# Attention with a gated feed-forward block on one core: loads and emission order redone

## The chip, the cores and the metric

One core of one Trainium2 chip runs the whole program. The metric is device time in microseconds (us). Every time quoted is a median of executions in the fast state. Traces are of one execution each, and their span (first to last instruction) is some 1.8 us below the time of that execution. Engines: PE is TensorE, PEld its weight loads, DVE VectorE, ACT ScalarE, POOL GpSimd, SP SyncE.

## The reference

```python
# q, k, v: (8, 8, 576, 64); phi: (8, 8, 576, 32)   [cut to what matters]
a = softmax(phi, axis=2)                     # over the 576 tokens, for each of 32 memory slots
k_m, v_m = a^T @ k, a^T @ v                  # per head 32 x 64
attn = softmax(q @ k_m^T / 8) @ v_m
x = attn in tokens x (heads * 64)            # 4608 x 512
out = (silu(x @ w_gate) * (x @ w_val)) @ w_out   # d_ff = 1536
```

The code works on eight batches of 576 tokens. For each it computes: the key/value sums ("sums"), the scores and their exponentials, the denominators, U = v_m @ w (so that the feed-forward input is never formed), 24 "slots" of gate and value matmuls with silu and multiply, and 54 output matmuls on average. In the kernels the softmax of phi runs over the tokens, with its denominator divided out of the sums. A U round (`u_round`) makes one piece of U of 512 columns, in eight matmuls and two copies. The exp chain is what stands between the scores and the first slot of a batch: exponentials, denominators and the division. In the profile lines t_qT is the transposed q, t_h the product of silu and value, t_A the divided exponentials, p_g and p_v the banks that scores, gates and values share, p_oo that of the outputs; L12 is line 12 of that kernel's file.

## The kernel before

```python
    def load_qT(b):

        t = att.tile([128, H, 3, P], BF16, tag="qT", name="t_qT")
        nc.sync.dma_start_transpose(
            out=t.rearrange("p h j t -> p (h j) t"),
            in_=qs[b].rearrange("p h f -> p (h f)"),
        )
        for i in range(NP):
            qTs[b, i] = t[:, 2 * i:2 * i + 2].rearrange("p h j t -> p h (j t)")
    # [cut]
    def load_w(which, c):
        src = (moe_w_gate, moe_w_val)[which]
        t = wpool.tile([128, NP, CH], BF16, tag=f"W{which}{c}", name=f"W{which}{c}")
        nc.gpsimd.dma_start(
            out=t, in_=src[:, c * CH:(c + 1) * CH].rearrange("(i p) f -> p i f", p=128)
        )
        W[which, c] = t
    # [cut: load_wo, key/value sums, q_T, scores, z_norm]
    def u_round(b, which, c):
        p = [ps.tile([128, CH], FP32, tag="s", name=f"p_u{g}") for g in range(NG)]
        for i in range(NP):
            for g in range(NG):
                nc.tensor.matmul(
                    p[g][32 * i:32 * i + 32, :],
                    lhsT=kTs[b][64 * g:64 * g + 64, 2, 32 * i:32 * i + 32],
                    rhs=W[which, c][64 * g:64 * g + 64, i],
                    start=True,
                    stop=True,
                    tile_position=(64 * g, 32 * i),
                )
        for g in range(NG):
            t = upool.tile([128, CH], BF16, tag=f"U{which}{c}{g}", name="t_U")
            if g == 0:
                nc.scalar.copy(out=t, in_=p[g])
            else:
                nc.vector.tensor_copy(out=t, in_=p[g])
            Us[b, which, c, g] = t
    # [cut]
    def gv_slot(b, s):
        jf, r = s // 2, s % 2
        c, o = jf // 4, jf % 4
        if b % 2 == 0 and r == 0:
            hts[b // 2, jf] = hpool.tile([128, 2 * S], BF16, tag=f"h{jf}", name="t_h")
        p = gv_banks()
        for which in range(2):
            for g in range(NG):
                nc.tensor.matmul(
                    p[which][:, 0:HALF],
                    lhsT=Us[b, which, c, g][:, 128 * o:128 * (o + 1)],
                    rhs=atts[b, g][:, r],
                    start=(g == 0),
                    stop=(g == NG - 1),
                )
        sg = work.tile([128, HALF], BF16, tag="sg", name="t_sg")
        nc.scalar.activation(out=sg, in_=p[0][:, 0:HALF], func=AF.Silu)
        flush_mul()
        col = (b % 2) * S + r * HALF
        dst = hts[b // 2, jf][:, col:col + HALF]

        def mul():
            nc.vector.tensor_tensor(out=dst, in0=sg, in1=p[1][:, 0:HALF], op=ALU.mult)

        pend.append(mul)
    # [cut: out_units, out_list]
    def att_items(b):
        q = [(330, lambda i=i: q_T(b, i)) for i in range(NP)] if b == 0 else []
        return (
            [(1000, lambda: (kv_half(b, 0), kv_half(b, 1), kv_sums(b)))]
            + q[:2]
            + [(200, lambda: kv_T(b))]
            + q[2:]
            + ([] if b == 0 else [(0, lambda: load_qT(b))])
        )
    # [cut]
    def window(b, fill, nxt_phi):
        lead = min(4, len(fill))
        run(fill[:lead])
        fill = fill[lead:]
        exp_tables()
        for g in range(NG):
            scores(b, g)
        if nxt_phi:
            phi_exp(b + 1)
        cut = len(fill) // 3
        run(fill[:cut])
        for g in range(NG):
            z_norm(b, g)
        run(fill[cut:])
    # [cut]
    backlog = []
    hold = {1: 0, 2: 12, 3: 12, 4: 14, 5: 14, 6: 16, 7: 0}
    for b in range(1, B):
        if b > 1 and b + 1 < B:
            load_phi(b + 1, nc.gpsimd)
            load_kv(b + 1)
            load_q(b + 1)
        n = min(36, len(backlog))
        window(b, backlog[:n], b > 1 and b + 1 < B)
        backlog = backlog[n:]
        keep = hold[b]
        rest, backlog = backlog[:len(backlog) - keep], backlog[len(backlog) - keep:]
        slots = [lambda s=s: gv_slot(b, s) for s in range(2 * NJF)]
        if b == 1:
            interleave(slots[:12], [])
            flush_mul()
            exp_tables()
            phi_exp(2)
            interleave(slots[12:], att_items(2) + u_items(2))
        else:
            nxt = att_items(b + 1) + u_items(b + 1) if b + 1 < B else []
            interleave(slots, rest + nxt)
        flush_mul()
        backlog += out_list(b)
    run(backlog)
```

q enters the scores transposed. For batch 0 PE transposes it; for batches 1 to 7 a DMA transpose (`load_qT`) does, issued by SP. GpSimd issues the other loads. The emission order is the order of each engine, but GpSimd may run ahead as far as buffers and semaphores let it.

The softmax here doesn't subtract the row's maximum and nothing guards it: scores larger than these inputs give would overflow.

## Time and profile before

| | before |
|---|---|
| time, median | 311.6 us (3 runs, 310.5 to 312.6) |
| PE busy | 253.5 us, 82% of the span |
| ACT, DVE busy | 175.3 and 154.2 us |
| PE waits for a DMA transpose | 11.2 us, once |
| start of the scores of batches 1 to 7, us | 77.1, 108.6, 139.0, 170.0, 202.3, 232.8, 265.0 |

How to read it: PE does nearly the same work in any order, so time is gained where PE stands still or runs at half clock. The starts of the scores, read from the timeline, cut the run into batches; from 108.6 to 265.0 a batch takes 31.3 us. The lines themselves are in the prediction, but for one from the list of who waited for whom (us in total, times, longest): the value matmul's wait for a multiply.

```profile
PE p_v L277 <- DVE t_h L291: 10.0, 27, 0.5
```

### The profile page before, as it was taken

How to read it: one execution, taken by the hardware profiler on the slowest of the kernel's cores; microseconds unless marked ns; L12 is line 12 of the kernel's file. 1: busy time of each engine (PE TensorE's matmuls, PEld its weight loads, DVE VectorE, ACT ScalarE, POOL GpSimd, SP SyncE). 2: the span in 40 equal slices, each digit the busy share in tenths (PEclk: the TensorE clock that was granted, in tenths of full speed). 3: DMA queues.
4: the chain of work that ended last, by engine and by line, in shares of the span. 5: the costliest groups of instructions: out<-in, count | busy, mean ns of one | idle time of the engine just before them, and what ended most of it. 6: DMA issues, size and time to landing. Idle time of an engine off the chain costs nothing.

```text
span 309.9 us, 5844 instructions
## 1 busy us (share of the span) xinstructions
PE 253.5 (82%) x2272; PEld 140.3 (45%) x2272; DVE 154.2 (50%) x326; ACT 175.3 (57%) x364; POOL 31.4 (10%) x46
## 2 busy tenths in 40 slices
PE   0278889520697899889988999999889998989994
PEld 0234454200353446534653466446544664456641
DVE  0135762330354736673667265836673567356520
ACT  4155672240866695569556944696569546845500
POOL 8222201100103010101010102000000000000000
PEclk9999999855588999999999999999999999999999
DMA  8999999999606933899399646945102270121133
GB/s 156 203 206 207 227 204 241 271 146 156 107 2 130 177 89 91 103 152 180 87 143 149 133 103 110 191 104 116 31 2 68 70 112 3 34 78 29 42 96 97
DMA packets 47499, 37.53 MB, mean 121 GB/s; under 512 B 18160, under 2 KB 41968, under 8 KB 47472
## 3 DMA queue, kind: packets, MB, share of 16 engines
q0 software_dynamic: 24576, 23.01, 45.6%
q1 hardware_dynamic: 22896, 14.16, 23.1%
q8 instruction: 17, 0.28, 0.4%
q14 instruction: 10, 0.08, 0.1%
HBM read 42.47 MB, written 9.44 MB: 167 GB/s over the span
## 4 chain that ended last, share of the span: by engine, by line
PE 65%; DVE 11%; DMA 10%; ACT 10%; issue 3%; POOL 0%; SPq 0%; DVEq 0%; ACTq 0%; POOLq 0%
PE p_oo L315 29%; PE p_v L277 14%; PE p_g L277 10%; PE p_u L245 7%; DMA t_qT<-t_q 6%; DMA t_q<-in_q_dram 4%; DVE t_h L291 4%; ACT t_U L256 3%; DVE t_U L258 3%; ACT t_lz L233 1%; ACT t_E L223 1%; PE p_kv L138 1%; ACT t_lz L232 1%; DVE t_o L327 1%; PE p_g L213 1%
## 5 line engine op out<-in xcount | busy, mean ns | idle before, releaser
L315 PE MATMUL p_oo<-WO,t_h 128*128 128x512 bf16 x432 | 109.7, 379 | 0.7 <-DVE t_o L327 0.7
L285 ACT ACTIVATE t_sg<-p_g 128x288 bf16<-128x288 f32 x192 | 77.5, 412 | 56.4 <-PE p_g L277 44.4
L291 DVE TENSOR_TENSOR t_h<-t_sg,p_v 128x288 bf16<-128x288 bf16 x192 | 83.9, 450 | 37.1 <-ACT t_sg L285 30.1
L277 PEld LDWEIGHTS <-t_U 128*128 128x128 bf16 x768 | 73.5, 100 | 61.2 <-issue 29.2
L277 PE MATMUL p_v<-t_A,t_U 128*128 128x288 bf16 x384 | 81.4, 295 | 10.9 <-DVE t_h L291 10.0
L277 PE MATMUL p_g<-t_A,t_U 128*128 128x288 bf16 x384 | 82.1, 296 | 3.5 <-DVE t_A L235 2.6
L315 PEld LDWEIGHTS <-t_h 128*128 128x128 bf16 x432 | 41.3, 98 | 39.9 <-issue 2.6
L256 ACT CAST t_U<-p_u 128x512 bf16<-128x512 f32 x48 | 28.1, 586 | 28.6 <-PE p_u L245 28.6
L258 DVE CAST t_U<-p_u 128x512 bf16<-128x512 f32 x48 | 33.2, 692 | 20.1 <-PE p_u L245 20.1
L235 DVE TENSOR_TENSOR t_A<-t_E,t_lz 128x576 bf16<-128x576 bf16 x16 | 12.1, 759 | 41.9 <-ACT t_lz L233 41.9
L327 DVE COPY t_o<-p_oo 128x512 f32<-128x512 f32 x28 | 19.1, 689 | 27.0 <-PE p_oo L315 27.0
L245 PE MATMUL p_u<-W,t_kT 64*32 64x512 bf16 x384 | 24.8, 421 | 9.1 <-ACT t_U L256 7.0
L245 PEld LDWEIGHTS <-t_kT 64*32 64x32 bf16 x384 | 8.4, 90 | 23.9 <-issue 19.4
L138 PE MATMUL p_kv<-t_kv,t_ephi 96*32 96x128 bf16 x384 | 7.6, 231 | 14.1 <-DMA t_kv<-in_v_dram 12.6
L223 ACT ACTIVATE t_E<-p_g 128x288 bf16<-128x288 f32 x16 | 6.6, 414 | 20.4 <-PE p_v L213 20.3
L124 ACT ACTIVATE t_ephi<-t_phi 96x768 bf16<-96x768 f32 x16 | 12.6, 844 | 3.8 <-DMA t_phi<-in_phi_dram 3.8
L213 PE MATMUL p_g<-t_qT,t_kT 64*32 64x288 bf16 x64 | 5.5, 324 | 11.3 <-DMA t_qT<-t_q 11.2
L377 ACT ACT_TABLE_LOAD x11 | 14.1, 1283 | 0.9 <-PEq L470 0.7
L325 ACT COPY t_o<-p_oo 128x512 f32<-128x512 f32 x8 | 4.7, 587 | 17.5 <-DMA out_dram<-t_o 9.8
L138 PEld LDWEIGHTS <-t_ephi 96*32 96x32 bf16 x384 | 6.0, 102 | 16.2 <-issue 14.2
L160 DVE RECIPROCAL t_rS<-p_kv 128x2 f32<-128x2 f32 x8 | 1.4, 170 | 21.2 <-PE p_kv L152 21.2
L72 POOL DMA_DIRECT2D t_kv<-in_k_dram x8 | 6.3, 785 | 54.1 <-PE p_kv L138 49.8
(37 smaller groups left out, 116.3 us busy)
## 6 DMA issues: line engine op xcount, KB each, us to landing
t_kv<-in_k_dram POOLq DMA_DIRECT2D x8, 576.0 KB, 11.3
t_kv<-in_v_dram POOLq DMA_DIRECT2D x8, 576.0 KB, 13.4
t_q<-in_q_dram POOLq DMA_DIRECT2D x8, 576.0 KB, 11.1
out_dram<-t_o SPq DMA_DIRECT2D x24, 192.0 KB, 2.3
t_phi<-in_phi_dram POOLq DMA_DIRECT2D x7, 576.0 KB, 6.6
out_dram<-t_o SPq DMA_DIRECT2D x24, 128.0 KB, 2.4
W<-in_moe_w_gate_dram POOLq DMA_DIRECT2D x3, 512.0 KB, 17.3
W<-in_moe_w_val_dram POOLq DMA_DIRECT2D x3, 512.0 KB, 19.1
```

The source lines that it names most:

```text
L124: nc.scalar.activation(out=t[:, :, g].rearrange("p j i m -> p i j m"), in_=src[:, g], func=AF.Exp)
L138: nc.tensor.matmul(pk[32 * i:32 * i + 32, 2 * D * g:2 * D * (g + 1)], lhsT=ephis[b][:, j, g, i], rhs=kvs[b][:, :, 2 * i + g, j * D:(j + 1) ...
L235: nc.vector.tensor_tensor(out=a, in0=e, in1=lz, op=ALU.mult)
L245: nc.tensor.matmul(p[g][32 * i:32 * i + 32, :], lhsT=kTs[b][64 * g:64 * g + 64, 2, 32 * i:32 * i + 32], rhs=W[which, c][64 * g:64 * g + 64 ...
L256: nc.scalar.copy(out=t, in_=p[g])
L258: nc.vector.tensor_copy(out=t, in_=p[g])
L277: nc.tensor.matmul(p[which][:, 0:HALF], lhsT=Us[b, which, c, g][:, 128 * o:128 * (o + 1)], rhs=atts[b, g][:, r], start=(g == 0), stop=(g = ...
L285: nc.scalar.activation(out=sg, in_=p[0][:, 0:HALF], func=AF.Silu)
L291: nc.vector.tensor_tensor(out=dst, in0=sg, in1=p[1][:, 0:HALF], op=ALU.mult)
L315: nc.tensor.matmul(mine["p"], lhsT=hts[c, jf][:, 128 * u:128 * (u + 1)], rhs=WO[jf], start=(jf == 0), stop=(jf == NJF - 1),)
L327: nc.vector.tensor_copy(out=t_o, in_=mine["p"])
L377: nc.scalar.preload_act_table_set("natural_log_exp_and_others")
```

## The change

It sends the loads in another order with W in halves, transposes q of batch 1 on PE, keeps U in single buffers that are filled just in time, emits a value matmul one slot after its gate, spreads output matmuls over the slots and the exp chain, and puts dummy matmuls into the start.

```diff
-    upool = ctx.enter_context(tc.tile_pool(name="upool", bufs=2))
+    upool = ctx.enter_context(tc.tile_pool(name="upool", bufs=1))
[cut: load_kv split into load_k and load_v]
+    HC = CH // 2
+    def load_w(which, c, half):
+
         src = (moe_w_gate, moe_w_val)[which]
-        t = wpool.tile([128, NP, CH], BF16, tag=f"W{which}{c}", name=f"W{which}{c}")
+        if half == 0:
+            W[which, c] = wpool.tile(
+                [128, 2, NP, HC], BF16, tag=f"W{which}{c}", name=f"W{which}{c}"
+            )
+        f0 = c * CH + half * HC
         nc.gpsimd.dma_start(
-            out=t, in_=src[:, c * CH:(c + 1) * CH].rearrange("(i p) f -> p i f", p=128)
-        )
-        W[which, c] = t
+            out=W[which, c][:, half],
+            in_=src[:, f0:f0 + HC].rearrange("(i p) f -> p i f", p=128),
+        )
 
     WO = {}
[cut: key and value sums split in two for batches 0 and 1; z_norm split into z_inv and norm]
-    def gv_slot(b, s):
+    def gv_half(b, s, which):
[cut]
+        gate = gv_half(b, s, 0)
         sg = work.tile([128, HALF], BF16, tag="sg", name="t_sg")
-        nc.scalar.activation(out=sg, in_=p[0][:, 0:HALF], func=AF.Silu)
+        nc.scalar.activation(out=sg, in_=gate, func=AF.Silu)
         flush_mul()
         col = (b % 2) * S + r * HALF
         dst = hts[b // 2, jf][:, col:col + HALF]
 
         def mul():
-            nc.vector.tensor_tensor(out=dst, in0=sg, in1=p[1][:, 0:HALF], op=ALU.mult)
+            val = gv_half(b, s, 1)
+            nc.vector.tensor_tensor(out=dst, in0=sg, in1=val, op=ALU.mult)
 
         pend.append(mul)
[cut]
+    def spread(*streams):
+
+        keyed = []
+        for o, (items, first, last) in enumerate(streams):
+            for i, x in enumerate(items):
+                keyed.append((first + (i + 0.5) * (last - first) / len(items), o, i, x))
+        for _, _, _, x in sorted(keyed, key=lambda t: t[:3]):
+            x()
[cut]
+    def warm(n):
+
+        p = ps.tile([128, DM], FP32, tag="o", name="p_oo")
+        for _ in range(n):
+            nc.tensor.matmul(p[:, 0:128], lhsT=bones, rhs=bones, start=True, stop=True)
[cut]
     load_phi(0, nc.sync)
-    load_kv(0)
+    load_k(0)
+    load_phi(1, nc.gpsimd)
     load_q(0)
-    make_identity(nc, ident)
+    load_v(0)
     nc.vector.memset(bones, 0.0)
     nc.vector.memset(ones1, 1.0)
     for h in range(4):
         nc.vector.memset(bones[32 * h:32 * h + 32, 32 * h:32 * h + 32], 1.0)
+    make_identity(nc, ident)
     for c in range(NCH):
-        for which in range(2):
-            load_w(which, c)
+        for half in range(2):
+            for which in range(2):
+                load_w(which, c, half)
+    load_phi(2, nc.gpsimd)
+    load_k(1)
+    load_q(1)
+    load_v(1)
     for c in range(3):
         load_wo(c)
-    load_phi(1, nc.gpsimd)
-    load_kv(1)
-    load_q(1)
+
 
     exp_tables()
     phi_exp(0)
-    run(att_items(0))
-    window(0, [], False)
-    u0 = u_items(0)
[cut: batch 0]
+    run(q_items(1)[:2] + k_items(1)[2:] + q_items(1)[2:])
+    load_k(2)
+    load_v(2)
[cut]
+            uw = u_items(b, "vv")
+            exp_tables()
+            run(take(2))
+            for g in range(NG):
+                scores(b, g)
+            run(take(6) + uw[2:3] + take(4))
+            if not last:
+                phi_exp(b + 1)
+            for g in range(NG):
+                z_inv(b, g)
+            nc.scalar.preload_act_table_set("silu_and_others")
+            run(take(4) + uw[3:4] + take(4))
+            norm(b, 0)
+            norm(b, 1)
+            run(take(8))
+        rest = take(len(backlog)) if last else take(len(backlog) - 28)
+        g = gv_slots(b)
+        streams = [(g, 0, 24), (rest, 0, 24)]
         if b == 1:
-            interleave(slots[:12], [])
-            flush_mul()
-            exp_tables()
-            phi_exp(2)
-            interleave(slots[12:], att_items(2) + u_items(2))
+            streams += [(u1[2:4], 1, 6), (u1[4:], 8, 14)]
         else:
-            nxt = att_items(b + 1) + u_items(b + 1) if b + 1 < B else []
-            interleave(slots, rest + nxt)
+            streams += [(u_items(b)[4:], 1, 8)]
+        if not last:
+            kvn = kv_items(b + 1)
+            streams += [
+                (kvn, 12, 17) if b == 1 else (kvn, 9, 15),
+                ([lambda: load_qT(b + 1)], 16, 17),
+                (u_items(b + 1)[:2], 18, 24),
+            ]
+        spread(*streams)
         flush_mul()
         backlog += out_list(b)
     run(backlog)
```

## The prediction

> **What bounds the kernel now.** I read four views in this order. First the page: slices of the span and the shares of the chain.
>
> ```profile
> span 309.9 us, 5844 instructions
> PE 253.5 (82%) x2272; PEld 140.3 (45%) x2272; DVE 154.2 (50%) x326; ACT 175.3 (57%) x364; POOL 31.4 (10%) x46
> ...
> PE   0278889520697899889988999999889998989994
> ...
> PEclk9999999855588999999999999999999999999999
> DMA  8999999999606933899399646945102270121133
> ...
> PE 65%; DVE 11%; DMA 10%; ACT 10%; issue 3%; POOL 0%; SPq 0%; DVEq 0%; ACTq 0%; POOLq 0%
> ```
>
> TensorE is the bound, but not everywhere. A slice is 7.75 us: PE is almost idle in the first two and again in the ninth and tenth (62 to 77 us), and just there the granted clock is 0.5. The DMA engines are full until about 78 us. The second view, the chain of waits from 56 to 78 us, and the third, the list of who waited for whom, name the hole:
>
> ```profile
> 57.03 19.98 DMA t_qT<-t_q
> ...
> 77.05 0.39 PE p_g L213
> ```
>
> ```profile
> PE p_g L213 <- DMA t_qT<-t_q: 11.2, 1, 11.2
> ```
>
> Batch 1's transposed q is made by a DMA transpose that takes 20.0 us; the median of the seven is 10.2 and the quickest 5.0. PE waits 11.2 us for it. The fourth view is the busy time by stage, here 66-77, 77-93, then a stretch of gate/value slots and an output stretch of a later batch:
>
> ```profile
> 66.00:77.00 11.00, 0.00 (x0) 0.00 (x0) 0.61 (x1) 1.76 (x2) 0.00 (x0) 0.50 1.37 144
> 77.00:93.00 16.00, 12.25 (x76) 7.18 (x75) 6.97 (x14) 11.81 (x25) 0.78 (x1) 0.67 0.38 62
> ...
> 118.00:138.00 20.00, 17.94 (x210) 10.95 (x208) 13.51 (x31) 11.66 (x29) 1.53 (x2) 1.00 0.81 113
> 138.00:149.00 11.00, 11.00 (x79) 5.48 (x72) 5.44 (x9) 9.30 (x17) 1.55 (x2) 1.00 0.87 175
> ```
>
> The columns are duration, busy us of PE, PEld, DVE, ACT, POOL, then clock, DMA share, GB/s. In 138-149, where output matmuls stand beside the exp chain, PE never stops. In 118-138 it has holes, which the timeline places at each U round:
>
> ```profile
> 129.51 0.41 PE L277 MATMUL p_g<-t_A,t_U 128*128 128x288 bf16 x2
> 130.28 0.41 PE L277 MATMUL p_v<-t_A,t_U 128*128 128x288 bf16 x2 [0.36 <-DVE t_h L291]
> 130.62 0.41 PE L245 MATMUL p_u<-W,t_kT 64*32 64x512 bf16 x8
> ```
>
> Value matmuls wait for a bank that a multiply frees, and the multiply stands behind a 0.69 us U copy. The period of "two slots and a U" is 1.95 us (128.67 to 130.62), the PE work in it 2 x 0.49 + 0.34 = 1.32.
>
> **What the Trainium skill says.** "TensorE: Matmul & The Clock Gate", Part 1 and "HAM oscillation": an idle window of about 3.4 us puts the clock at half, and a busy window restores it. The trace agrees: 0.50 in 66-77, and pairs of slots take 0.96 us instead of 0.49 until 87. "DMA: Bandwidth & Descriptors", "Queues, rings and completion order": each of the 16 engines goes round robin between queues by packet, and work already queued on another queue is therefore shared with, not passed. The trace agrees: 5.0 us with nothing else under way, 20.0 us beside the loads of batches 2 and 3. "ScalarE: Activation LUTs", "What ACT_TABLE_LOAD costs": about 1283 ns for the load itself; the trace has 1.28 us.
>
> **Unit costs on PE**, all from the trace at full clock. Output matmul 0.216 (48 in 10.37 us, chain of waits from 45.11). A slot 0.49 (four matmuls, 0.245 per pair). U round 0.34 (128.67 to 129.01). Key/value sums 1.1 (125.13 to 126.23) and transposes 0.3. Scores and denominators 1.05 a batch (the gaps 139.08 to 139.63 and 141.90 to 142.38 between output stretches).
>
> **Part 1, the start.** Landings before, issue plus time to landing: k0 9.6, v0 12.5, q0 15.4, the six W by 30.7, WO by 38.3, q1 49.7, k2 55.3, v2 59.7, q2 66.3. Steps are 2.9 us for a k, v or q, about 2.6 for a phi, 2.55 for a W or WO; this is a stream at full rate. The change sends the same bytes in another order. I estimate: q0 15, v0 18, W halves (I take 1.28 each) 20 to 33.5, phi1 now early, phi2 36, k1 39, q1 42, v1 45, WO 47.5 to 52.5, k2 55.5, v2 58, q2 61. The dummy matmuls keep the clock up while PE waits for q0. Before, the first silu of batch 0 is at 27.2 and its slots end at 45. After, v0 (18) and the first W half (20) still stand in PE's order ahead of the denominators, so the first silu is near 25; a group of four slots with two half U's costs DVE 4 x 0.49 + 2 x 0.4 = 2.8 us, so 24 slots take about 17 and end near 42.
>
> **Part 2, batch 1.** q is transposed on PE, so the 20 us transfer is off this place. Its chain (exp table 1.28, phi exp 1.57, copies, exps 1.3, log and exp 2.7, two U rounds with 4 x 0.69 of copies on DVE) from 42 puts its first slot near 52, against 82 before: 30 us earlier. But output matmuls that filled 45 to 55 move too. Only 20 of the first 48 are put beside batch 1's slots and 28 are held. So not all of the 30 us is won.
>
> **Part 3, batch 2, where I expect the wait to come back.** Its q is still transposed by DMA. The order of SP shows it behind the stores of the first output tile, which completes at the 12th of 20 output matmuls, about slot 14: 52 + 14 x 0.85 = 64. GpSimd runs ahead with loads: at 64 to 65 the queue still has part of v3, q3, phi4, and k4, v4 as soon as batch 2's sums free their buffer: 2 + 2.9 + 2.6 + 2.9 + 2.9 = 13.3 us of loads. With 5 us for the transpose that is 18 to 20, as for the 20.0 of before. It lands near 85. The slots of batch 1 (24 x 0.49 + 20 x 0.216 + 4 x 0.34 + 1.4 + two U rounds 0.7 = 19.5, some 21 with bubbles) end near 74 and two output matmuls later PE stands in order before the scores of batch 2: about 10 us idle, and a half clock after it. Before, these scores were at 108.6, with 52 output matmuls done; now at 85 with 22 done. Net of 30 x 0.216 = 6.5 that is 17 us won, not 24.
>
> **Part 4, batches 2 to 7.** PE work from 85 on: 410 outputs x 0.216 = 88.6; 144 slots x 0.49 = 70.6; 34 U rounds x 0.34 = 11.6; sums 5 x 1.4 = 7; scores 6 x 1.05 = 6.3. Sum 184. The end (last copy and store, 305.6 to 309.9 before) is 4.3. Losses: before, 138.1 to 264.1 holds four batches of which PE's work is 4 x 16.2 + 212 x 0.216 = 111, so 3.8 a batch was lost. In the change the value is one slot behind its gate, so its multiply finds the silu done; outputs are spread over all slots, so U rounds stand beside them. I leave 0.3. In the window the ACT chain is table 1.3 + exps 1.3 + phi 1.6 + logs 2.6 + table 1.3 = 8.1, against 28 x 0.216 + 1.05 + 0.68 = 7.8 of PE work: 0.5 lost. So 0.8 x 6 = 5, and 3 for the half clock after the wait. Later DMA transposes are issued at slots 9 to 14 and have at least 9 us; I count nothing.
>
> 85 + 184 + 4.3 + 5 + 3 = 281 of span; the runs before are 1.7 above their span: 283. I add 1 for small stalls: **284 us**.
>
> **Rivals.** (a) The transpose of batch 2 is not in the way: if its loads are issued later or share better, scores come at 75 and the time is about 274. For it: uncontended it takes 5 us. Against: the DMA is full until the loads have caught up, and nothing in the change thins it. (b) The half chunks halve the bytes per run to 512; if the engines pay per run, W takes 4 to 5 us more and all behind it moves: 288 to 290. The spacing of 768 and 1024 byte runs (2.9 us for 576 KB, 2.55 for 512) is by bytes, against it. (c) Single U buffers and both copies on DVE make DVE the bound: DVE has 17 us in slots of 20, so it would cost 1 to 2 a batch: 290 to 296. (d) All steady losses vanish and the start goes as planned: 268 to 272.
>
> **Range and chances.** (a) and (d) set the low end, 271; (b) with (c) the high end, 296. For no gain, 27 us of stall would have to be new, and I see no place: faster by over 2% has 0.97.
>
> **What would show it.** Right: the granted clock full until about 45; first slot of batch 1 near 52; a PE wait of 6 to 13 us for the DMA transpose before batch 2's scores near 75 to 86, with half clock; then a period of 28 to 29 us a batch instead of 31; the value matmul's wait for the multiply gone. Wrong if that transpose lands by 75 (faster), if the W halves land later than 36, if PE waits for DVE in the slots, or if later transposes hold up scores.

## The result, and the profile after

292.75 us median (291.5 to 294.9, 4 runs) against 311.06 for the kernel before beside it: ratio 0.941 (95% interval 0.934 to 0.949). A second measurement gave 294.02 against 312.24 (three fast runs; 294.75 with a fourth that was slow), ratio 0.9415. The prediction was 284 with a range of 271 to 296.

The page of the changed kernel: span, busy shares, the 40 slices of 7.3 us, and the chain by engine.

```profile
span 293.0 us, 6428 instructions
PE 254.7 (87%) x2504; PEld 148.6 (51%) x2538; DVE 165.9 (57%) x350; ACT 168.6 (58%) x354; POOL 36.0 (12%) x52
...
PE   7587997699439998599959999799999999999993
...
PEclk9655999799959999689997999999999999999999
DMA  7999999999979179572797439970512251211233
...
PE 64%; DMA 23%; ACT 6%; DVE 3%; issue 2%; POOL 0%; ACTq 0%; POOLq 0%
```

The one deep hole of before has become several: PE falls in slices 11 and 12, in 17 and in 21, and each time the clock falls with it or just after. DMA has gone from 10% to 23% of the chain. (Slice 1 shows 7 because of the dummies.) The list of who waited for whom:

```profile
PE p_g L274 <- DMA t_qT<-t_q: 17.0, 4, 8.3
PE p_g L349 <- DVE t_A L303: 4.0, 4, 1.6
...
PE p_u L316 <- DVE t_U L333: 0.9, 2, 0.7
```

17.0 us in four waits for a transposed q: 8.3, 3.9, 3.3 and 1.6. The value matmul's wait for the multiply, 10.0 us in 27 waits before, has gone from the list. The chain of waits has the four transposes: start, length.

```profile
70.52 14.54 DMA t_qT<-t_q
...
105.01 15.44 DMA t_qT<-t_q
...
144.46 9.45 DMA t_qT<-t_q
...
173.01 13.75 DMA t_qT<-t_q
```

They are those of batches 2 to 5. What GpSimd issues at the second of them:

```profile
104.51 0.77 POOL L72 DMA_DIRECT2D t_kv<-in_k_dram  x1 [15.06 <-PE p_kv L149]
105.27 0.77 POOL L76 DMA_DIRECT2D t_kv<-in_v_dram  x1
```

The sums of batch 3 free a key/value buffer, and the two loads that waited for it start in the same microsecond as the transpose. Busy time by stage (length, then busy us of PE, PEld, DVE, ACT, POOL, clock, DMA share, GB/s): the wait of batch 2, its slots, the wait of batch 3.

```profile
77.00:85.20 8.20, 0.10 (x8) 0.11 (x16) 0.07 (x1) 0.65 (x1) 0.00 (x0) 0.79 1.13 139
94.50:116.00 21.50, 21.11 (x220) 13.51 (x222) 14.82 (x33) 12.46 (x30) 1.53 (x2) 1.00 0.69 97
116.00:120.50 4.50, 0.60 (x8) 0.11 (x5) 0.72 (x2) 1.20 (x1) 0.00 (x0) 0.88 0.83 127
```

In the slots PE is busy 21.1 of 21.5 us; before, it was 17.9 of 20 in a like stretch. The timeline of PE at a U round shows how:

```profile
98.59 0.41 PE L349 MATMUL p_v<-t_A,t_U 128*128 128x288 bf16 x2
98.84 0.38 PE L396 MATMUL p_oo<-WO,t_h 128*128 128x512 bf16 x1
...
99.15 0.41 PE L316 MATMUL p_u<-W,t_kT 64*32 64x512 bf16 x8
99.49 0.39 PE L396 MATMUL p_oo<-WO,t_h 128*128 128x512 bf16 x1
99.72 0.41 PE L349 MATMUL p_g<-t_A,t_U 128*128 128x288 bf16 x2
99.96 0.41 PE L349 MATMUL p_v<-t_A,t_U 128*128 128x288 bf16 x2
```

None has a bracket, which would give idle time before it; the prediction's like lines of the kernel before have 0.36 us of wait just before the U round.

### The profile page after: what moved, and what is told of

It is laid out like the page before. It is cut to its first block, busy times and chain, and to the rows that moved or that the text cites. A ratio compares the mean times of both kernels' runs of the same rounds, so it can differ in the third digit from the quotient of the medians.

```text
span 293.0 us, 6428 instructions
## 1 busy us (share of the span) xinstructions
PE 254.7 (87%) x2504; PEld 148.6 (51%) x2538; DVE 165.9 (57%) x350; ACT 168.6 (58%) x354; POOL 36.0 (12%) x52
## 4 chain that ended last, share of the span: by engine, by line
PE 64%; DMA 23%; ACT 6%; DVE 3%; issue 2%; POOL 0%; ACTq 0%; POOLq 0%
PE p_oo L396 25%; DMA t_qT<-t_q 18%; PE p_g L349 15%; PE p_v L349 13%; PE p_u L316 5%; DMA t_q<-in_q_dram 4%; PE p_kv L149 2%; ACT t_lz L297 2%; PE p_g L274 1%; ACT L563 1%; DVE t_U L333 1%; ACT t_lz L298 1%; DVE t_A L303 1%; PE p_q L251 1%; PE p_kv L161 1%
## 5 line engine op out<-in xcount | busy, mean ns | idle before, releaser
L396 PE MATMUL p_oo<-WO,t_h 128*128 128x512 bf16 x398 | 119.6, 393 | 2.1 <-issue 1.0
L372 DVE TENSOR_TENSOR t_h<-t_sg,p_v 128x288 bf16<-128x288 bf16 x192 | 86.6, 454 | 45.7 <-PE p_v L349 42.1
L349 PE MATMUL p_v<-t_A,t_U 128*128 128x288 bf16 x384 | 79.6, 291 | 0.1
L333 DVE CAST t_U<-p_u 128x512 bf16<-128x512 f32 (+1 forms) x70 | 42.9, 632 | 13.4 <-PE p_u L316 12.7
L331 ACT CAST t_U<-p_u 128x512 bf16<-128x512 f32 (+1 forms) x38 | 20.1, 530 | 10.9 <-PE p_u L316 10.4
L316 PE MATMUL p_u<-W,t_kT 64*32 64x512 bf16 (+1 forms) x432 | 23.2, 381 | 1.6 <-DVE t_U L333 0.9
L82 POOL DMA_DIRECT2D t_q<-in_q_dram x8 | 6.2, 773 | 60.0 <-DMA t_qT<-t_q 56.4
L297 ACT ACTIVATE t_lz<-p_g 128x288 f32<-128x288 f32 x16 | 6.4, 402 | 8.9 <-PE p_g L294 8.8
L460 PE MATMUL p_oo<-bones 128*128 128x128 bf16 x98 | 10.0, 295 | 1.5 <-DVE bones L471 1.5
L298 ACT ACTIVATE t_lz<-t_lz 128x576 f32<-128x576 f32 x16 | 10.9, 684 | 0.5
```

What stands on the lines that cost most here:

```text
L297: nc.scalar.activation(out=lz[:, r], in_=p[r][:, 0:HALF], func=AF.Ln)
L298: nc.scalar.activation(out=lz, in_=lz, func=AF.Exp, scale=-1.0)
L316: nc.tensor.matmul(p[g][32 * i:32 * i + 32, f0:f1], lhsT=kTs[b][64 * g:64 * g + 64, 2, 32 * i:32 * i + 32], rhs=w, start=True, stop=True, ...
L331: nc.scalar.copy(out=t[:, f0:f1], in_=p[g][:, f0:f1])
L333: nc.vector.tensor_copy(out=t[:, f0:f1], in_=p[g][:, f0:f1])
L349: nc.tensor.matmul(p[:, 0:HALF], lhsT=Us[b, which, c, g][:, 128 * o:128 * (o + 1)], rhs=atts[b, g][:, r], start=(g == 0), stop=(g == NG - 1),)
```

## The experiments

Twelve measurements (eleven kernels and the change once more), in three sets of four. The first two sets ran on one chip, the third on another, each with runs of the kernel before beside it (medians 311.3 to 312.2); the first two rows are from the measurement of the change. Starts of the scores (us, from the timelines), the time and the ratio to before:

| kernel | batch 1 | 2 | 3 | 4 | 5 | 6 | 7 | time | ratio (95%) |
|---|---|---|---|---|---|---|---|---|---|
| before | 77.1 | 108.6 | 139.0 | 170.0 | 202.3 | 232.8 | 265.0 | 311.06 | 1 |
| after | 46.6 | 85.1 | 120.5 | 154.0 | 186.8 | 214.3 | 244.4 | 292.75 | 0.941 (0.934-0.949) |
| qT_early | 44.9 | 84.7 | 117.2 | 144.8 | 174.9 | 202.5 | 232.6 | 282.24 | 0.902 (0.895-0.909) |
| qT_early_from_b2 | 44.4 | 83.8 | 116.3 | 143.9 | 174.0 | 201.6 | 231.7 | 280.79 | 0.898 (0.890-0.905) |
| q2_on_pe | 44.7 | 76.6 | 107.4 | 138.0 | 170.7 | 198.3 | 228.3 | 277.22 | 0.887 (0.880-0.894) |
| value_with_gate | 44.2 | 83.7 | 117.0 | 148.5 | 180.4 | 209.2 | 239.8 | 289.24 | 0.925 (0.918-0.932) |
| loads_held_back | 44.5 | 74.2 | 104.2 | 131.9 | 161.9 | 189.5 | 219.6 | 270.32 | 0.864 (0.857-0.872) |
| q2_on_pe_qT_early | 45.2 | 77.3 | 107.3 | 134.9 | 165.0 | 192.6 | 222.7 | 272.90 | 0.873 (0.866-0.879) |
| no_warm | 43.5 | 84.4 | 116.0 | 146.4 | 178.4 | 205.9 | 235.9 | 288.35 | 0.923 (0.915-0.931) |
| outputs_bunched | 43.8 | 82.7 | 114.4 | 143.0 | 173.4 | 201.9 | 232.3 | 286.00 | 0.912 (0.904-0.921) |
| after_again | 44.5 | 84.4 | 119.0 | 151.5 | 184.1 | 211.6 | 241.7 | 294.02 | 0.9415 (0.936-0.947) |
| held_back_no_warm | 45.9 | 76.2 | 106.3 | 133.9 | 164.0 | 191.6 | 221.6 | 272.55 | 0.873 (0.871-0.876) |
| held_back_value_with_gate | 45.7 | 78.8 | 109.4 | 138.2 | 168.8 | 197.7 | 228.2 | 277.73 | 0.889 (0.885-0.892) |
| before_q1_on_pe | 68.1 | 100.7 | 131.3 | 162.1 | 194.4 | 224.9 | 257.2 | 304.33 | 0.975 (0.972-0.978) |

All results were correct.

**Theory:** what keeps the change from its steady rate is that a DMA transpose shares the DMA engines with key and value loads that are in the queue, and PE stands before the scores until it lands. **Rival:** the transpose is slow of itself, or SP issues it too late.

### qT_early: the transpose at slot 0

```diff
-                ([lambda: load_qT(b + 1)], 16, 17),
+                ([lambda: load_qT(b + 1)], 0, 1),
```

> The DMA transpose of the next batch's q is emitted at slot 0 instead of slot 16.5, so it no longer starts together with the key and value loads that the key/value sums release. My theory (the transpose shares the DMA engines packet by packet with those loads, and PE stands before the scores until it lands): the waits before the scores of batches 3, 4 and 5 (8.7 us in the changed kernel) vanish, that of batch 2 shrinks from 8.3 to about 3, and the half clock after each goes too; about 275 us against 293, the ratio to before near 0.885. Rival (the transpose is slow of itself or the SP queue holds it wherever it stands): the waits stay near 17 us and the time within 2 of 293.

282.24 us, 7 above the expectation. The waits of batches 3 to 5 are gone: those transposes land 5.0 to 6.6 us after issue instead of 9.4 to 15.4. But batch 2's did not come earlier. The list of waits, and the chain:

```profile
PE p_g L274 <- DMA t_qT<-t_q: 9.6, 1, 9.6
```

```profile
61.72 22.91 DMA t_qT<-t_q
```

It is issued 8.8 us earlier than in the changed kernel and lands at 84.6 instead of 85.1. So the theory holds for batches 3 to 5, and the size for batch 2 was wrong: with loads queued ahead and behind, the place of the transpose in the order hardly counted. What stretches it is counted under loads_held_back.

### qT_early_from_b2: the same, batch 2 left alone

```diff
+                ([lambda: load_qT(b + 1)],) + ((16, 17) if b == 1 else (0, 1)),
```

> The same, but batch 2's transpose is left where it was. My theory: batch 2's wait of 8 us stays, those of batches 3 to 5 vanish (8.7 us and some 3 of half clock): about 281 us. If the wait of batch 2 is what sets all the later ones (a delay that is handed on), they stay: 290 or more.

280.79, as expected. Batch 2's wait is 9.2 us, the others are gone: a wait is not handed on, and the early issue did nothing for batch 2.

### q2_on_pe: batch 2's q on TensorE

```diff
-        pq = ps.tile([128, NG, HALF], BF16, tag="gv"[i % 2], name="p_q")
+        pq = ps.tile([128, NG, HALF], BF16, tag=("s" if b > 1 else "gv"[i % 2]), name="p_q")
...
+                (q_items(2), 18, 22) if b == 1 else ([lambda: load_qT(b + 1)], 16, 17),
```

> Batch 2's q is transposed on TensorE in the last slots of batch 1 instead of by DMA; all else as in the change. My theory: the 8.3 us wait before the scores of batch 2 is replaced by about 1 us of PE work, and its half clock goes: about 283 us, with the waits of batches 3 to 5 still there. Rival (PE would wait there for the loads anyway): q lands at about 63 us, slot 18 is at about 70, so no wait for it; if there is one, the time stays near 290.

277.22, 6 us better than expected. The scores of batch 2 start at 76.6 instead of 85.1. The expectation had left the waits of batches 3 to 5 as they were; here they are 3.8 us in two instead of 8.7 in three.

### value_with_gate and held_back_value_with_gate: one part undone

```diff
         gate = gv_half(b, s, 0)
+        val = gv_half(b, s, 1)
         sg = work.tile([128, HALF], BF16, tag="sg", name="t_sg")
...
         def mul():
-            val = gv_half(b, s, 1)
```

> Undoes one part: value matmuls are issued in the same slot as their gate, as before. By my prediction the value's wait for the multiply comes back: up to 0.6 us for each U round that stands in slots, 4 a batch, so up to 2.4 us a batch or 14 us in all; 300 to 307 us. Rival (the output matmuls spread over the slots fill that time anyway, and the DMA waits absorb what is left): within 3 us of 293.

289.24: undoing the part made the kernel faster than the change at 292.75 (and its repetition at 294.02, on another chip). The list of waits says why this says nothing on the part itself:

```profile
PE p_g L274 <- DMA t_qT<-t_q: 10.1, 3, 6.4
...
PE p_v L349 <- DVE t_h L372: 1.4, 5, 0.3
```

The waits for transposes fell from 17.0 to 10.1 us as slots and transposes met at other moments, which hides what the part is worth. So it was undone once more in loads_held_back (below), where no such wait is left:

> loads_held_back with the value matmuls back in the slot of their gate. In the undisturbed pairs of batches value_with_gate took 59.4 us against 57.7 (scores to scores), 0.85 a batch; over six batches 5 us: 275 to 276. If the part is worth nothing: 270. If my prediction's size for it was right (1.5 to 2.4 a batch): 279 to 284.

277.73, ratio 0.889 against 0.864 with the part. From the scores of batch 3 to those of batch 7 there are 118.9 us here (109.35 to 228.20), and 115.4 in loads_held_back (104.24 to 219.60): 0.9 us a batch. The slots of batch 1 add about 2.4 (52.4 to 78.0 against 50.0 to 73.2, by the first and last gate or value matmul). So the part is worth about 0.9 us a batch in the steady stage, less than the 1.5 to 2.4 of my prediction's size, and in the change as it stands none of it is visible.

### loads_held_back: one buffer for k, v and q

```diff
-        t = inp.tile([P, 2, H, J * D], BF16, tag="kv", name="t_kv")
+        t = inp.tile([P, 2, H, J * D], BF16, tag="kv", bufs=1, name="t_kv")
...
-        t = inp.tile([P, H, J * D], BF16, tag="q", name="t_q")
+        t = inp.tile([P, H, J * D], BF16, tag="q", bufs=1, name="t_q")
...
-                ([lambda: load_qT(b + 1)], 16, 17),
+                ([lambda: load_qT(b + 1)], 0, 1),
```

> Key/value and q tiles get one buffer instead of two, so batch 3's loads cannot start before batch 2's data are used up, and batch 2's transpose, emitted at slot 0, has the DMA engines nearly to itself from about 62 to 67 us. In qT_early, with two buffers, it was issued at 61.7 and landed at 84.6. My theory (it is the backlog of loads in the queue that stretches it): it lands by about 70, the 9 us wait before the scores of batch 2 vanishes, and the time falls from 282 to about 270 although less is prefetched. Rival (the backlog is only part, or the later loads now come too late): a wait of 5 us or more stays at batch 2's scores, or new waits for k, v or q appear, and the time is 280 or more.

270.32, the best of all. The DMA issues between 61 and 66 us (size, median us to landing), in qT_early and then here:

```profile
t_kv<-in_k_dram POOLq DMA_DIRECT2D x1, 576.0 KB, 20.3
t_qT<-t_q SPq DMA_TRANSPOSE x1, 22.9
```

```profile
t_kv<-in_k_dram POOLq DMA_DIRECT2D x1, 576.0 KB, 9.4
t_kv<-in_v_dram POOLq DMA_DIRECT2D x1, 576.0 KB, 12.1
t_qT<-t_q SPq DMA_TRANSPOSE x1, 6.5
```

The same transpose, issued at 62.2 instead of 61.7, took 6.5 us instead of 22.9. Between the two kernels only the buffers differ, and with them which loads may start. After 60 us PE's list has no wait for a DMA of any kind. This settles theory against rival: it is the backlog. How the engines were shared can be counted in the two DMA queues of qT_early from 66 to 82 us, q0 with the loads that GpSimd issued, q1 with what SP issued (packets, MB, share of the engines):

```profile
q0 software_dynamic: 1979, 1.97, 91.1%
q1 hardware_dynamic: 1981, 0.51, 44.7%
```

The two queues moved as many packets, one for one, but those of the transpose have some 260 bytes and those of the loads 1.0 KB, so the transpose got a fifth of the bytes. In loads_held_back q1 moved 2334 packets from 63 to 67 us, with 17 of q0 beside them.

### q2_on_pe_qT_early: the other mend

Both edits above together.

> Both mends together: batch 2's q transposed on TensorE, the later DMA transposes at slot 0. My theory: no wait for a transpose is left; 277.2 less the 3.8 us of waits and a half clock of about 3 that q2_on_pe still has: about 270 us. If the gains do not add: 275 to 277.

272.90: no wait for a transpose either, and 2.6 us behind loads_held_back in the same rounds. Batch 2's scores start 3.1 us later, with PE doing 24 transposes more in batch 1's slots.

### no_warm and held_back_no_warm: without the dummy matmuls

```diff
-    warm(60)
...
-    warm(30)
...
-    warm(8)
```

> The changed kernel without its 98 dummy matmuls. My theory: the time from batch 2 on is set by the DMA transpose, so nothing of the start reaches the end: within 2 us of the changed kernel (about 293), though the first slots of batch 0 run at half clock for longer. Rival (the dummies are worth what they warm): 3 to 8 us slower.

288.35. As with value_with_gate, its waits for transposes are fewer (12.3 us in three), so it does not measure the dummies.

> loads_held_back (270.3) without the dummy matmuls; here no transpose wait hides a later start. My theory, from the clock records (with dummies the clock falls back to half from 10 to 14 and 21 to 28 us, without them no half clock is recorded before 51): they gain nothing, 269 to 271. Rival: they are worth what they warm and their lack is now visible: 273 or more.

272.55, ratio 0.873 against 0.864, so by the ratio some 1% slower, between the two cases. But the two sets ran on different chips, and here q0 came later: the scores of batch 0 start at 17.3 us, as in held_back_value_with_gate on that chip (17.4), which has the dummies; in loads_held_back it was 15.9. From there to the scores of batch 2 it is 58.9 us without and 58.3 with dummies. The reason given in the expectation was wrong: the first record of the clock comes late in a trace (29.8 us here), and before it pairs of gate matmuls start 0.9 us and more apart, that is at half clock, just as with the dummies. In the changed kernel the dummies bring full clock at 6.7 us, and it is gone at 10.1 while PE waits for k (3.2 us). A gain beyond 0.6 us is not shown; exactly zero isn't either.

### outputs_bunched: output matmuls in the first 8 slots

```diff
-        streams = [(g, 0, 24), (rest, 0, 24)]
+        streams = [(g, 0, 24), (rest, 0, 24 if last else 8)]
```

> The output matmuls beside the slots are put into the first 8 of the 24 slots instead of all 24; nothing else changes. My theory (spreading them fills the holes that U copies and the multiply leave in later slots): the last 16 slots become bound by ScalarE and VectorE at about 0.54 instead of 0.49 us, and U rounds there cost up to 0.6 each: 1.5 to 2.5 us a batch, 8 to 14 us in all, of which the DMA waits of batches 2 to 5 may absorb half: 297 to 305. Rival (the value one slot behind already removes the holes): within 2 us of 293.

286.00, a miss in sign: faster than the change. The list of waits names the cause:

```profile
PE p_g L274 <- DMA t_qT<-t_q: 8.3, 1, 8.3
```

SP issues in order, so a transpose stands behind the stores of an output tile that is emitted before it. With outputs bunched the tile is done sooner: batch 3's transpose is issued at 102.5, 3.2 us before the next loads instead of between them, and takes 5.2 us instead of 15.4. Those of batches 3 to 5 land in time, and only batch 2's wait is left. Against qT_early_from_b2 (280.79, same chip, another set), which also has that wait alone, bunching costs some 5 us. From the scores of batch 5 to those of batch 7 it is 58.9 us against 57.7 there: 0.6 a batch.

### before_q1_on_pe: one part of the change alone

```diff
-        q = [(330, lambda i=i: q_T(b, i)) for i in range(NP)] if b == 0 else []
+        q = [(330, lambda i=i: q_T(b, i)) for i in range(NP)] if b < 2 else []
...
-            + ([] if b == 0 else [(0, lambda: load_qT(b))])
+            + ([] if b < 2 else [(0, lambda: load_qT(b))])
```

> The kernel before with one part of the change alone: batch 1's q transposed on TensorE too, so that nothing waits for the 20 us DMA transpose at 57 to 77 us. Theory A (most of the change's gain is that one wait of 11.2 us and the half clock after it): 294 to 298. Theory B (the wait moves on to batch 2's transpose, which now meets the same loads): 303 or more.

304.33, ratio 0.975: a gain of 8 us, below A. The number is B's, the reason isn't: the only wait for a transpose in PE's list is 0.2 us, before the scores of batch 3. All scores come 8 to 9 us earlier, from batch 1 to batch 7. What now stands before the scores of batch 1 are its six U rounds, which start 1.46 us apart from 60.45 to 67.75, most after 0.69 us of wait for a U copy, and the clock is at half from 61.7 to 78.8 us; that this is why no more is won was not tested. The list of waits still has the loss in the slots that the change removes:

```profile
PE p_v L277 <- DVE t_h L291: 9.9, 27, 0.5
```

### after_again: the change once more

> The changed kernel itself once more, beside the others on their chip, because value_with_gate, no_warm and outputs_bunched all came out 4 to 7 us below its 292.75, which was taken elsewhere. If that is the chip or the draw: 286 to 290 here, and those three runs say nothing against the parts that they undo. If the parts really cost time: 292 to 294 again.

294.02 in the three fast runs, ratio 0.9415, so the change is what it was. The three kernels that undo a part are faster than the change by ratios whose intervals do not meet its own, though each part by itself is worth something or nothing. Their gain lies in fewer or shorter waits for transposes. Why value_with_gate's and no_warm's batch 3 transposes land in 13.5 and 10.6 us and the change's in 15.4 was not tested.

## Why the prediction was right or wrong

The range held and the direction was right; the median is 9 us above the 284 predicted.

**What held.** The mechanism of Part 3 is what happened: batch 2's transpose was to land near 85, with about 10 us of idle PE; its scores start at 85.1 after a wait of 8.3. qT_early and loads_held_back showed that the reason was the right one. That the landing fits so well is partly luck: it was to be issued at 64 and take 18 to 20 us, and was issued at 70.5 and took 14.5. By Part 2, batch 1's first slot was to be near 52; it is at 52.4, again by two misses that cancel: batch 0's slots end at 44.2 instead of 42, and the chain after them takes 8.2 us instead of 10. W in halves costs little: the last half lands at 34.8, against 33.5 predicted, so rival (b) is out. Rival (c) is out too: PE waits for DVE 1.8 us before the first slots of batch 1 and never after 55 us.

**What did not.** The clock was to be full until about 45, kept up by the dummies. It was at half from 10.1 to 30.6; the first silu still came at 25.9, against 25. Two details of the working are off as well: 0.96 and 0.49 us are for one slot, not for a pair, and 8.1 against 7.8 is 0.3 lost in the exp chain, not 0.5 (1 us over six batches).

**The step that failed** is a term of Part 4: "Later DMA transposes are issued at slots 9 to 14 and have at least 9 us; I count nothing." Batch 3's was issued at 105.0, at about slot 12, and PE came to its scores at 116.6, so it had 11.6 us, but it took 15.4. The room was right and the length was not: the sums of batch 3 let two loads go in the same microsecond. Batches 3 to 5 then waited 3.9, 3.3 and 1.6, 8.7 us in all; "if later transposes hold up scores" was one of the prediction's own signs of being wrong. The profile before had the sign of it, as transposes that started together with loads took 10.2 and 12.8 us and those without took 5.0 and 5.9; I used that for batch 2 and not for the others.

**The sum.** The half clock after the waits was put at 3 us for one wait. By the clock record of the changed kernel's trace it stood at half from 81.8 to 88.7, 119.4 to 126.2 and 153.5 to 156.9 us. Counted from where the scores start that is 3.6, 5.7 and 2.9, 12.2 us, in which PE does half the work: up to 6 us lost by this estimate, 3 more than I put. 281 of span as predicted, and 8.7, and 3: 293; the span of the trace is 293.0. That it fits to a tenth is luck: the other terms were not measured one by one, and the traced run, 294.86, is the slowest of the four.

**What was hidden.** Where nothing waits, the period is that of Part 4: in loads_held_back batches 3 to 7 start 28.8 us apart (115.4 over 4), where 28 to 29 was predicted and 31.3 is what before takes. In the change the mean from batch 2 to 7 is 31.9. So the steady gain of some 2.4 us a batch was there and was spent in the waits: what the change shows is the earlier scores of batch 2, 85.1 against 108.6 with 30 output matmuls (6.5 us) fewer done, which is 17 us, as much as the two spans differ by (309.9 and 293.0). Of this, batch 1's q on PE alone gave 8 us in before_q1_on_pe. How the rest divides between load order, the order in the exp chain and the output matmuls put off was not separated.

**Which mechanism removed the slots' loss** was put on two things. The value's delay is worth about 0.9 us a batch, the spreading about 0.6; I had the two near 3 in sum (3.8 a batch before, 0.8 left), and the holes at U rounds are indeed gone, so each may cover for the other in part. That leaves about 0.9 of the 2.4 us a batch, which the new order in the exp chain may have given. Undoing both at once, or that order alone, was not tried.

## What to carry to other kernels

A prefetch that runs as far ahead as buffers allow can lengthen the one transfer that is wanted next; fewer buffers, so that a load cannot start before the urgent transfer is through, gave 12 us here (282.24 to 270.32). Before judging a part by undoing it, look whether a wait elsewhere absorbs its effect: three parts looked harmful in the change, and where transposes held up less, two of them were worth 0.9 and 0.6 us a batch and the third (the dummies) nothing that could be shown. Compare the landing time of each DMA with and without neighbours, not its median.

## What the Trainium skill lacked or had wrong

- "DMA: Bandwidth & Descriptors", "Latency and other measured facts", gives 261 GB/s for a DMA transpose; the rules at its end say that a transpose next to ordinary DMAs needs nothing. The second is meant for correctness, and no run contradicts it. For the time beside loads the page has no figure: the same 576 KB transpose took 5.0 us from issue to landing alone, 9.4 to 15.4 with key and value loads under way, 22.9 in front of a full queue, and 6.5 when the next loads were held back.
- "DMA: Bandwidth & Descriptors", "Queues, rings and completion order", tells the round robin by packet, which agrees with the packets counted in qT_early (1979 and 1981 from the two queues in 16 us). It does not say what follows for a transpose, whose packets of some 260 bytes got a fifth of the bytes beside packets of 1.0 KB, nor for order: issuing the transpose 8.8 us earlier moved its landing by 0.5 us (84.6 against 85.1).
- "TensorE: Matmul & The Clock Gate", Part 1, puts the full clock some 4 us into sustained matmuls and the half clock after an idle window of about 3.4 us. In the changed kernel the dummies began at 1.5 us and the clock was full at 6.7; it was at half again at 10.1, only 2.6 us after the last of the first dummies ended (7.5), and 4.7 us of PE work without a pause from 10.7 did not bring it back; it was full again at 30.6. What the page doesn't tell is how much work in a window is enough, either way.
- Part 1 warns that clock records in a trace can be unreliable, but no page says that they may begin late with half clock before them: the first is at 29.6 us in the kernel before and 29.8 in held_back_no_warm, and until then gates of successive slots start 0.9 us and more apart. The PEclk line of the profile shows 9 in those slices all the same.
